# A gated outer-product recurrence and a token-channel mixer on one core: f loaded by token pairs, prefix sums from 64-row products, joint masks, scalings and exponentials

## The chip, the core and the metric

The kernel runs on 1 core of one Trainium2 chip. The metric is device time in microseconds (us) of one launch. Engines are named as in the profile: PE (TensorE matmuls), PEld (its weight loads), DVE (VectorE), ACT (ScalarE), POOL (GpSimd), SP (SyncE, which here only issues DMAs). PSUM has 8 banks of 512 float32 columns; the kernel hands them out by number.

## What is computed

For 4 batches of 768 tokens, 8 heads and 48 channels per head, a linear recurrence with a forget gate, and on its result a mixer over tokens and then over channels:

```python
f = 1.0 / (1.0 + np.exp(-f_logit))
for t in range(S):
    state = f[:, :, t, :, None] * state + np.einsum('bhd,bhe->bhde', k[:, :, t], v[:, :, t])
    y[:, :, t] = np.einsum('bhd,bhde->bhe', q[:, :, t], state)
x = y.transpose(0, 2, 1, 3).reshape(B, S, H * D)
h = np.maximum(x.transpose(0, 2, 1) @ w_tok1, 0.0) @ w_tok2
u = x + h.transpose(0, 2, 1)
out = u + np.maximum(u @ w_ch1, 0.0) @ w_ch2
```

## The kernel before

Each batch is cut into six chunks of 128 tokens. In a chunk, L = ln(1 + exp(-f_logit)) is made on ACT and split into a bfloat16 upper half (`Lhi`, a view) and a remainder (`Llo`, made by a subtraction on DVE or POOL). A product with a triangle of ones gives the prefix sums over the chunk's tokens in a PSUM bank. ACT turns the bank into the two gates G = exp(-sum) and Gi = exp(+sum); DVE scales q by G and k by Gi; PE transposes both; the copies out of PSUM are called *turned*. The score matmuls put a chunk's 8 heads into two banks, DVE multiplies them by the triangular mask, and two more products give y: *within* (masked scores by v) and *past* (q by the block-diagonal copy of the state, `state_bd`, which the helper `spread` makes). *parts* is k by v, the chunk's share of the next state. The result is copied out twice, as `x_bf` and `x_nat`. The mixer then runs *tok1* and *tok2* (over tokens), a transpose *ut*, and *ch1* and *ch2* (over channels), 288 matmuls of 128x384 per direction of the channel part over the whole kernel.

**Batch 0** goes by pairs of chunks (`pair(m)`, m = 0, 1, 2). Its loads put two consecutive tokens into each partition, so that partition t of column j holds token 2t + j of 256, and partitions 0 to 63 hold the first chunk of the pair, 64 to 127 the second. The masks for this layout are `pmask`. **Batches 1 to 3** go by `attention(b, (c, c + 1))` with one token per partition; there `sums_and_turns` makes the prefix sums by two matmuls of 128x384 per chunk (L461 with `Lhi`, L462 with `Llo`).

Nothing is scheduled at run time. The helper `add` records every operation with its engine, `ORDER` is a list of their numbers with an engine letter and the PSUM banks to use, and `plan.run` writes the instructions in that order. Each engine works through its own part of the list in order; semaphores between engines are put in when the program is built, from the tiles and the PSUM banks that two instructions share. So what matters around the change is the list and those waits. The DMAs of q, k, v, f of batch 1 and the weights are issued from POOL's part of the list (L266, L272), f of batch 0 and the stores from SP's.

Lines of before that the prediction uses: L392 and L388 make L of batch 0 and L371, L372 that of the others; L628 and L630 are G and Gi of batch 0; L637 scales q or k of batch 0, L490 both at once in the others; L644 transposes and L676 scores of batch 0; L706 is its mask; L665, L719 and L743 are parts, within and past of batch 0; L277 and L279 are copies on ACT and DVE; L413 and L500 are scores and transposes of the other batches; L757, L773, L826, L845 are tok1, tok2, ch1, ch2; L877 and L882 are idle matmuls at the start.

Of the kernel before, what the change touches and what calls it, by code (L numbers as in the profile page):

```python
# [28 lines left out]
HALVES = False  # L29
STATES = (DVE, POOL,)  # L30
# [6 lines left out]
w512 w512 w384 s19 32 20G 7G 33 8D 6G 10D 0D 34 11G 19D 1 5D 9G 2 24D 3A 27D 23A 18D 21G 22G 35 49 37 50 16G 51 36 52D  # L37
54 14D 13D 25D 12D 53G 26A 55 28 39 100:0 58 56D 105:1 40 57D 102 59 38 104 137:2 101 60D 142:3 42 108 107 61D 106 110
41 139 109 119:1:0 144 103 114:4 29D 143 62 111:5 125 138 115 112 116D 180:1 113A 130 146 126A 140 117:0:4 30A 127G
148:5 43 31A 149 141 175:2 181 147 121 145 150A 131G 118:3:6 120 44 151:0 176 123 156:5:4 182 17G 152 177 122 15G 153A  # L40
185 63 124:2:3 179 184 183 134 133A 178 189:6 64 132A 190 162 186:1 191A 187 4G 154:5:0 45 157 188A 163G 158 155:6:0 46
129A 169 193:1:5 164A 160 135A 47 128D 165A 192:4:6 159 339 65 336 197 161:2:0 337 170G 195 340 166 338G 198 342 194:5
173 172A 196 171G 358:1 343 341G 200 199:6:7 360 167D 359 201G 215:5 136D 204 361 216 203G 366:4 205D 202G 208:3 362
174A 217 68 363 209 206 367 210 168D 364:1 369 67 207D 211 218 345 212 365D 213 66 219 220 214A 374:2 221D 368 242 72
238 377 243 239 222:5 244D 234 241A 344G 235 226:1 240A 378 227 256:4 236A 230:3 70 254:6 257D 231 245A 228 252:2 394:4
255A 69 253D 223 346 248:7 232 290:6 249A 224 73 288:2 396 229 291A 284:7 233 347G 250:1 286:6 285A 251D 351 48 246:3
402:1 397 247D 300:7 225 76 352 289D 270:3 405 301D 264:5 74 272:2 406 237A 348 296:7 71 370 273D 268:0 349 398 271D 75
265A 292:2 269D 297A 276:3 371 287A 266:7 350D 403 258:6 353D 395 298:0 267A 81 277D 404 262:4 293A 372:3 439:2 373D
382:1 260:7 299D 79 375:5 261A 376:0 386 259A 78 304:7 263A 407 302:5 385 441 294:4 384A 379 280:6 295A 383D 381G 274:3
440 380G 387 278:4 399 431:0 281D 388G 282:2 432 275D 391:6 279A 469:1 283A 400:3 393D 433 408:4 392A 77 326:2 390A 409D  # L50
434 306:6 389G 303D 435 401D 327 305D 410:5 411:0 413 412:7 328 415 414 470 321:3 416D 436 417A 307 423 418G 82 437:5
424 419:0 329 462:7 83 422 322 421A 330 438A 420D 308 425G 427G 463 323 80 445:0 324 85 587 331:4 449 596 332 584 86 309
585 464 448 310 428:6 426G 590 311:0 87 429D 333 442 430A 84 586D 593 443:5 588 334 354 447:6 444D 602:3 454:4 605 450
471 451D 446:2 606 589D 594 316:6 604 457 312 452G 603 89 458 453A 610:5 591 607 472 465 88 611 459:2 595D 612 608:3
592D 455A 313 613 460D 466 615 473 597 474 456D 467 646:5 468A 598G 475D 317 647 314 609A 479:1 91 461D 482:7 488:0 480
649 476:2 483 616:4 481G 648 477 491:1 484G 599 638:7 489 95 478A 496:2 492 485:5 640 318 497D 617A 92 486 498:2 494:1
620:0 490G 499A 495D 618:5 319 600 90 619:1 622 493A 508:2 96 520:6 623 509A 630 518:5 639 601G 621 830 528:2 641 510:1
631 487G 521D 506:0 642 624G 821 629 625G 526:6 614 507A 94 519D 522:7 824 643 502:0 831 93 524:5 527D 529A 512:4 833
503D 97 635:2 818 513D 514:0 511A 98 819 504:4 516:6 505D 834 820D 644:1 356 517A 515D 500:4 525A 626:3 675:6 651 501A
554:5 678 637D 548:4 636D 679 677 652:0 632G 645D 628A 650 555 355 827 523D 676 653D 559:2 549A 627D 634A 546:6 656:4  # L60
547A 655:3 633G 659 825 654:7 822 836:6 657 556 823G 666 683:1 667 560 660G 685 832G 828 658 552:0 839 532:3 557 99
536:7 680 661A 684 713:5 662G 561 553A 686 838 542:1 537D 357 672:0 562 544:7 668 673D 663:2 545A 687:4 669D 543A 665D
843:7 837 538:1 674D 826G 846 533D 530:6 847 845 671G 714 534:3 531D 844 840 681:0 688D 539A 535A 706:7 707 664D 550:1
682D 540:2 551A 691:3 541A 689:6 694 690:1 670A 693 870:2 695G 574:3 692 873 697G 575 696G 702 874 829G 576 701 841 715
708 698:4 577 871 877:1 835D 709 703:3 848 569:0 699D 849 878 570 704D 872 700D 716 717 710 842 718 711 905:4 719D 712A
852:2 705A 732:5 558 855 879 735:7 320 880 856G 723:3 736 563 729:6 857A 726:1 733 881 737G 908 571 730 325 724 579:5
# [9 lines left out]
1006:0 983D 978:4 977D 996:1 1010:7 990:6 1011D 992:3 991D 968:7 997D 993A 1004:6 979D 1012:1 1005D 970:4 1015D 998:6  # L76
969D 986:5 973D 1002:7 999D 1000:2 971D 1003A 1008:6 1007D 987A 1046:7 1013D 1031:5 1001D 1036:1 1009D 1037 1041:6
1021:2 1047 1032 1048 1022 1038 1023 1039 1042 1049 1024 1050 1043 792 1026:2 1040 1016:7 1033 1017 1034 1027 1044 1035
1045 1028 1025 1018 1029 1030 1019 1020
"""  # L80


# [833 lines left out]
```

## Time and profile before

| | |
|---|---|
| median of 3 runs | 172.35 us (171.44 to 172.51) |
| the profiled execution | 172.62 us, its span 169.8 us |
| PE busy | 161.6 us of the span, 1757 matmuls |
| DVE, ACT, POOL busy | 130.1, 101.1, 86.7 us |
| mean granted TensorE clock | 0.976 |
| DMA | 89572 packets, 22.72 MB |

The span runs from the first to the last instruction; 2.8 us of the execution lie around it. The profile's page cuts the span into 40 slices of 4.2 us and gives the busy share of each engine in tenths. Three stretches can be told apart. In the first 25 us batch 0 is worked off by a chain over all engines, and PE has gaps. From there to 166 us PE is never idle: the mixer of one batch and the attention of the next are interleaved. The last 3.5 us are the last sum on DVE and the last stores.

### The profile page before, as it was taken

The numbers are of one execution on the slowest core, as the hardware profiler recorded it, in microseconds if no ns is written. First come the engines' busy times: TensorE is split into PE (matmuls) and PEld (weight loads), VectorE is DVE, ScalarE is ACT, GpSimd is POOL, SyncE is SP. The second block draws the span as 40 slices with busy tenths as digits, with TensorE's granted clock in tenths as the row PEclk, the third lists the DMA queues.
The fourth block names the chain that finished last, engine by engine and source line by source line (L and its number), as shares of the span: only waits on it lengthen the run. The fifth ranks groups of instructions, "written<-read, shape, count | busy, mean of one in ns | idle before, by whom it ended". The sixth has DMA issues, their size and how long they took to land.

```text
span 169.8 us, 4441 instructions
## 1 busy us (share of the span) xinstructions
PE 161.6 (95%) x1757; PEld 103.9 (61%) x1757; DVE 130.1 (77%) x282; ACT 101.1 (60%) x226; POOL 86.7 (51%) x125
## 2 busy tenths in 40 slices
PE   6799789999999999999999999999999999999991
PEld 2476556566676666666667665666657665666660
DVE  4389796998789799998989897999677426687222
ACT  3999997789671759999977737656541223112000
POOL 8899989899461997899989131110120010000000
PEclk9999956999999999999999999999999999999998
DMA  5999999999999999999999929995340033700044
GB/s 140 235 171 220 204 179 210 189 137 178 172 226 151 88 139 159 194 102 61 87 140 145 127 11 111 277 209 168 62 108 4 0 70 73 276 4 0 0 148 178
DMA packets 89572, 22.72 MB, mean 134 GB/s; under 512 B 82288, under 2 KB 88736, under 8 KB 89552
## 3 DMA queue, kind: packets, MB, share of 16 engines
q0 software_dynamic: 69600, 13.77, 95.6%
q1 hardware_dynamic: 19952, 8.69, 20.2%
q8 instruction: 13, 0.21, 0.5%
q14 instruction: 7, 0.06, 0.1%
HBM read 25.17 MB, written 4.72 MB: 176 GB/s over the span
## 4 chain that ended last, share of the span: by engine, by line
PE 88%; ACT 5%; DVE 2%; DMA 2%; issue 0%; DVEq 0%
PE ps L826 28%; PE ps L845 28%; PE ps L757 5%; PE ps L773 5%; PE ps L500 3%; PE ps L413 3%; PE ps L461 2%; PE ps L564 2%; DMA f_sb<-in_f_logit_dram 2%; PE ps L462 2%; PE ps L429 2%; PE ps L560 2%; DVE zT L706 1%; PE ps L644 1%; PE ps L719 1%; ACT f_sb L392 1%
## 5 line engine op out<-in xcount | busy, mean ns | idle before, releaser
L845 PE MATMUL ps<-w_ch,zT 128*128 128x384 bf16 (+2 forms) x300 | 52.1, 320 | 0.0
L826 PE MATMUL ps<-uT,w_ch 128*128 128x384 bf16 x288 | 52.0, 326 | 0.0
L845 PEld LDWEIGHTS <-zT 128*128 128x128 bf16 x300 | 28.0, 98 | 17.1
L826 PEld LDWEIGHTS <-w_ch 128*128 128x128 bf16 x288 | 27.2, 97 | 17.3
L357 ACT ACTIVATE zT<-ps 128x384 bf16<-128x384 f32 x48 | 22.3, 491 | 20.6 <-PE ps L826 16.8
L359 DVE TENSOR_SCALAR zT<-ps 128x384 bf16<-128x384 f32 x48 | 24.8, 550 | 2.8 <-PE ps L826 2.7
L541 DVE TENSOR_TENSOR AmT<-ps,tri_bf 128x512 bf16<-128x512 f32 x36 | 23.4, 683 | 0.9 <-PE ps L413 0.7
L851 DVE TENSOR_TENSOR x_nat<-x_nat,ps 128x384 f32<-128x384 f32 (+2 forms) x25 | 12.8, 533 | 11.4 <-PE ps L845 11.3
L281 POOL CAST state_bd<-state 48x192 bf16<-48x192 f32 x24 | 8.6, 357 | 23.9 <-DVE state L577 9.5
L266 POOL DMA_DIRECT2D qk_sb<-in_q_dram x16 | 15.6, 979 | 1.1 <-DMA w_ch<-in_moe_w_ch_dram 1.1
L266 POOL DMA_DIRECT2D v_sb<-in_v_dram x16 | 15.8, 990 | 0.5 <-DMA f_sb<-in_f_logit_dram 0.5
L266 POOL DMA_DIRECT2D qk_sb<-in_k_dram x16 | 16.0, 1000 | 0.1
L789 DVE TENSOR_TENSOR x_nat<-x_nat,ps 128x384 f32<-128x384 f32 x21 | 10.6, 548 | 4.9 <-PE ps L773 4.9
L757 PE MATMUL ps<-x_bf,w_tok 128*128 128x384 bf16 x48 | 13.0, 340 | 0.0
L279 DVE CAST x_bf<-ps 128x384 bf16<-128x384 f32 x18 | 9.9, 552 | 3.7 <-ACT x_nat L277 1.7
L281 POOL CAST u_bf<-x_nat 128x384 bf16<-128x384 f32 x8 | 4.3, 544 | 16.2 <-issue 11.4
L471 ACT ACTIVATE GG<-ps 128x384 bf16<-128x384 f32 x18 | 8.7, 489 | 5.2 <-DVE qk L490 3.6
L490 DVE TENSOR_TENSOR qk<-qk_sb,GG 128x768 bf16<-128x768 bf16 x18 | 10.0, 556 | 0.3 <-ACT GG L471 0.3
L773 PE MATMUL ps<-h1T,w_tok 128*128 128x384 bf16 x48 | 9.8, 326 | 0.0
L473 ACT ACTIVATE GG<-ps 128x384 bf16<-128x384 f32 x18 | 8.8, 491 | 1.6 <-PE ps L462 1.2
L379 POOL TENSOR_TENSOR Llo<-L 128x384 bf16<-128x384 f32 x10 | 8.3, 833 | 2.0 <-ACT L L372 2.0
L372 ACT ACTIVATE L<-f_sb 128x384 f32<-128x384 f32 x18 | 9.1, 523 | 0.2
(103 smaller groups left out, 262.0 us busy)
## 6 DMA issues: line engine op xcount, KB each, us to landing
out_dram<-x_nat SPq DMA_DIRECT2D x23, 192.0 KB, 2.2
f_sb<-in_f_logit_dram POOLq DMA_DIRECT2D x3, 1152.0 KB, 10.8
f_sb<-in_f_logit_dram SPq DMA_DIRECT2D x3, 384.0 KB, 4.2
qk_sb<-in_k_dram POOLq DMA_DIRECT2D x12, 96.0 KB, 7.4
qk_sb<-in_q_dram POOLq DMA_DIRECT2D x12, 96.0 KB, 6.2
w_ch<-in_moe_w_ch_dram POOLq DMA_DIRECT2D x2, 576.0 KB, 11.8
v_sb<-in_v_dram POOLq DMA_DIRECT2D x12, 96.0 KB, 5.1
w_ch<-in_moe_w_ch_dram POOLq DMA_DIRECT2D x1, 1152.0 KB, 9.5
```

The lines of the kernel that those rows point to most:

```text
L266: lambda eng=eng, into=into, of=of: eng.dma_start(out=into, in_=of),
L281: nc.gpsimd.tensor_copy(out_, in_)
L357: nc.scalar.activation(out_, in_, AF.Relu, bias=0.0, scale=1.0)
L359: nc.vector.tensor_scalar(out_, in_, 0.0, None, ALU.max)
L490: add(("gated", b, c, *names), DVE, lambda n=n: nc.vector.tensor_tensor(qk[it][:, n, :, 0:D], qk_sb[nb][:, n, :, c, :], GG[i][:, n], ALU.m ...
L541: add(("masked", b, c, p), DVE, lambda half=half, made=made: nc.vector.tensor_tensor(half, made(), tb4, ALU.mult), need=["tri_bf"], make=[ ...
L757: add(("tok1", b, rt, kt), PE, lambda rt=rt, kt=kt, pm=pm: nc.tensor.matmul(banks[pm.at][:, 0:DM], lhsT=w_tok1[:, kt, rt * 128:(rt + 1) * ...
L773: nc.tensor.matmul(banks[pm.at][:, 0:DM], lhsT=w_tok2[:, kt, tt * 128:(tt + 1) * 128], rhs=h1T[:, kt, :], start=(kt == 0 and not held), st ...
L789: nc.vector.tensor_tensor(to, un, banks[pm.at][:, 0:DM], ALU.add)
L826: nc.tensor.matmul(banks[pm.at][:, 0:384].rearrange("p (n t) -> p n t", t=128), lhsT=w[:, kt, c0:c0 + 128], rhs=uT[:, rows3, kt, :], start ...
L845: nc.tensor.matmul(banks[pm.at][:, 0:n1 - n0], lhsT=zT[:, kt, tt * 128:(tt + 1) * 128], rhs=w_ch2[:, kt, n0:n1], start=(kt == 0), stop=(kt ...
L851: add(("sum", b, tt, n0), DVE, lambda un=un, pm=pm, n=n1 - n0: nc.vector.tensor_tensor(un, un, banks[pm.at][:, 0:n], ALU.add), make=[("x_n ...
```

## The change

It has four parts and a new `ORDER`.

1. **f of batches 1 to 3** is loaded by token pairs like batch 0's (`FPAIR`): 384 contiguous bytes instead of 192, half as many descriptors.
2. **Their prefix sums** come from products of 64 rows. The upper 64 partitions of a column hold the first chunk of a pair, the lower 64 the second; the two triangles needed (`steps[:, 0]`, `steps[:, 1]`) are the masks that batch 0 already had. For two chunks there are 8 matmuls with 64 rows and 384 columns, alternately rows 0 to 63 into one bank and 64 to 127 into another, in place of 4 with 128 rows.
3. **In batch 0** the scaling of q and k of a chunk is one DVE instruction of 768 columns (`GATED2`), and the mask of a chunk one of 1024 columns over its two banks (`MASK2`).
4. **In pairs 1 and 2 of batch 0** G of both chunks is one ACT instruction over two banks, and Gi too (`EXP2`). For this `GG` is one tile, and all eight banks are one PSUM tile `ps`; two banks x < y are read as `psum[:, x:y + 1:y - x]`.

`HEADS`, `HALF0` and `COPIED` are off, so their branches make nothing.

```diff
+GATED2 = (0, 1, 2)
+MASK2 = (0, 1, 2)
+EXP2 = (1, 2)
+FPAIR = True
...
-w512 w512 w384 s19 32 20G 7G 33 8D 6G 10D 0D 34 11G 19D 1 5D 9G 2 24D 3A 27D 23A 18D 21G 22G 35 49 37 50 16G 51 36 52D
+w512 w512 w512 s7 32 18G 33 5D 20D 34 14D 7D 21D 0D 12D 1 6G 2 36 23D 3D 26D 24D 22G 27D 28 49 8D 13G 17D 35 29D 50 37
...
-    GG = [st([128, 2, H, D], BF16, f"GG{i}") for i in range(2)]
+    GG2 = st([128, 2, 2, H, D], BF16, "GG")
+    GG = [GG2[:, i] for i in range(2)]
...
-    banks = [ps.tile([128, 512], FP32, tag=f"ps{i}", name=f"ps_{i}") for i in range(NBANK)]
+    psum = ps.tile([128, NBANK, 512], FP32, tag="ps", name="ps")
+    banks = [psum[:, i] for i in range(NBANK)]
...
+            if b and n == "f" and FPAIR:
+                into = into.rearrange("t h (m j) d -> t h m (j d)", j=2)
+                of = src[b].rearrange("h (m t j) d -> t h m (j d)", t=C, j=2)
...
     def attention(b, cs):
         nb = b % NB
-        heads = [sums_and_turns(b, c) for c in cs]
+        p_s = [Bank(), Bank()]
+        if FPAIR:
+            c0 = cs[0]
+
+            def prefix():
+                for n, (t, j) in enumerate((t, j) for j in range(2) for t in (Lhi[b % 2][:, c0 + j], Llo[place(b, c0 + j)])):
+                    for k in range(2):
+                        rows = slice(64 * k, 64 * k + 64)
+                        nc.tensor.matmul(banks[p_s[k].at][:, 0:DM], lhsT=steps[rows, j, :], rhs=t[rows, :, 0:D],
+                                         start=(n == 0), stop=(n == 3))
...
+            def both(n, scale):
+                (x, y) = sorted(b.at for b in p_s)
+                of, for_ = psum[:, x:y + 1:y - x, 0:DM], GG2[:, :, n].rearrange("p j h d -> p j (h d)")
+                nc.scalar.activation(for_, of, AF.Exp, bias=0.0, scale=scale)
...
+            if m in GATED2:
+                add(("gated", 0, c), DVE, lambda j=j, c=c: nc.vector.tensor_tensor(
+                    qk[j][:, :, :, 0:D], qk_sb[0][:, :, :, c, :], GG[slot(j)], ALU.mult),
+                    need=[("q", 0, c), ("k", 0, c), ("G", j), ("Gi", j)], make=[("qh", j), ("kh", j)],
+                    kind=("el", 2 * DM, False, 2))
...
+            def masked(j=j):
+                x, y = p_a[j][0].at, p_a[j][1].at
+                nc.vector.tensor_tensor(
+                    ATp[i2][:, j].rearrange("p (r n) t -> p r n t", r=2),
+                    psum[:, x:y + 1:y - x].rearrange("s r (n t) -> s r n t", t=C),
+                    pmask[j].rearrange("s t j -> s (t j)").unsqueeze(1).unsqueeze(1).broadcast_to((128, 2, 4, C)), ALU.mult)
```

The new list gives these pairs of banks to the joint instructions of batch 0. Exponentials: 0 and 2 for pair 1, 0 and 6 for pair 2. Masks of chunks 1, 0, 3, 2, 4, 5, in their order on DVE: 4 and 5, 2 and 3, 1 and 6, 2 and 5, 1 and 4, 3 and 6.

What the list does to the order is shown at three places, each row with the semaphores that the instruction waits for; a semaphore is named after the engine that raises it (Activation is ACT). The first is ACT in before, at the exponentials of pair 2, which come in four instructions with the copies of pair 1 (`zT<-ps`) between and after them:

```order
L628 ACTIVATE GG_81<-ps_113 128x384 [waits DVE_49,PE_49]
L633 ACTIVATE gpair_121<-ps_115 128x8
L277 ACTIVATE zT<-ps_117 128x1024 [waits PE_49]
L628 ACTIVATE GG_80<-ps_114 128x384 [waits DVE_49,PE_49]
L630 ACTIVATE GG_81<-ps_113 128x384 [waits DVE_49]
L630 ACTIVATE GG_80<-ps_114 128x384
L277 ACTIVATE zT<-ps_112 128x1024 [waits DVE_49,PE_49]
```

The same place now, on ACT:

```order
L301 ACTIVATE zT<-ps 128x1024 [waits PE_49]
L301 ACTIVATE state_bd_96<-state 48x4x48 [waits DVE_49,Pool_49]
L301 ACTIVATE steps<-x_nat_100 64x64
L694 ACTIVATE GG<-ps 128x2x384 [waits DVE_49,PE_49]
L694 ACTIVATE GG<-ps 128x2x384 [waits PE_49,Activation_49]
L301 ACTIVATE zT<-ps 128x1024
L301 ACTIVATE zT<-ps 128x1024 [waits PE_49]
```

Two joint exponentials stand ahead of both copies of pair 1, and each has a wait for PE. Counted through the semaphores' raises in the compiled program, the first waits for the mask of chunk 1 on DVE (banks 4 and 5) and the scores of chunk 0 on PE (banks 3 and 2), the second for the transposes of k of chunks 2 and 3 on PE (bank 1); all these banks lie between 0 and 6.

The second place is DVE in before, from the third mask of pair 1 to the last of pair 2:

```order
L706 TENSOR_TENSOR zT<-ps_118,x_nat_101 128x512 [waits PE_49,Activation_49]
L279 CAST x_bf_102<-ps_114 128x384 [waits Activation_49]
L706 TENSOR_TENSOR zT<-ps_112,x_nat_101 128x512
L706 TENSOR_TENSOR zT<-ps_117,x_nat_101 128x512 [waits PE_49]
L706 TENSOR_TENSOR zT<-ps_118,x_nat_101 128x512 [waits PE_49]
L706 TENSOR_TENSOR zT<-ps_113,x_nat_101 128x512
L706 TENSOR_TENSOR zT<-ps_116,x_nat_101 128x512 [waits PE_49]
```

And DVE there now, from the mask of chunk 3 to that of chunk 5:

```order
L778 TENSOR_TENSOR zT<-ps,steps 128x1024 [waits PE_49,Activation_49]
L303 COPY zT<-ps 128x1024 [waits PE_49]
L778 TENSOR_TENSOR zT<-ps,steps 128x1024 [waits PE_49,Activation_49]
L778 TENSOR_TENSOR zT<-ps,steps 128x1024 [waits PE_49]
L846 TENSOR_TENSOR tsum<-state,ps 128x192 [waits PE_49,Pool_49]
L778 TENSOR_TENSOR zT<-ps,steps 128x1024 [waits PE_49]
```

Four joint masks stand where seven rows were; counted the same way, the first waits on ACT for the `x_nat` copy of chunk 0 (bank 2, between 1 and 6), the second for a turned copy of pair 2 (bank 4, between 2 and 5), the last on PE for *within* of chunks 2 and 3 (it writes banks 2 and 5; 5 lies between 3 and 6).

The third place is PE now, at the transposes of k of chunks 2 and 3, behind the scores of chunk 0:

```order
L760 MATMUL ps<-zT 64x128
L726 LDWEIGHTS qk_81 [waits DVE_49]
L726 MATMUL ps<-ident,qk_81 128x128 [waits Activation_49]
L726 LDWEIGHTS qk_81
L726 MATMUL ps<-ident,qk_81 128x128
```

In before the transposes of q of chunk 4 stood at the like place of the next pair, behind *past* of chunk 1:

```order
L743 LDWEIGHTS zT
L743 MATMUL ps_115<-state_bd_97,zT 128x96
L644 LDWEIGHTS qk_82 [waits DVE_49]
L644 MATMUL ps_118<-ident,qk_82 128x128
L644 LDWEIGHTS qk_82
```

The wait on ACT in the new rows is for the first joint exponential of pair 2 (banks 0 and 6), while the transposes write bank 1. On PE there also stand now: the transposes of k of chunks 4 and 5 (bank 3) with a wait for the mask of chunk 3 (banks 1 and 6); the scores of chunk 4 into bank 4 with a wait for the mask of chunk 2 (2 and 5); *within* of chunks 2 and 3, from bank 2 on, with one for the mask of chunk 4 (1 and 4); and *past* of chunk 3 (bank 5) with one for the mask of chunk 5 (3 and 6).

More of the change, by code (lines that the diff above doesn't have):

```diff
@@ L42 @@
[L42 to L46, printed above, removed]
@@ L204 @@
     tsum = st([128, HP, D], FP32, "tsum")
+    state_bf = [st([128, HP, D], BF16, f"state_bf{i}") for i in range(2)] if HEADS else None
     state_bd = [st([128, HP, 2 * D], BF16, f"state_bd{i}") for i in range(2)]
```

186 lines of the change are left out of this document (134 added, 52 removed).

## The prediction

> **What bounds the kernel now.** I read the page first, for the span and the slices.
>
> ```profile
> span 169.8 us, 4441 instructions
> PE   6799789999999999999999999999999999999991
> DVE  4389796998789799998989897999677426687222
> ACT  3999997789671759999977737656541223112000
> PEclk9999956999999999999999999999999999999998
> ```
>
> PE is full from the seventh slice to the last but one. So the end is set by when PE becomes full, by the work left for it then, and by its clock. Two digits of the clock, 5 and 6, stand in slices 6 and 7. The chain that ended last confirms it: from the first tok2 on it is PE alone, and it ends with one sum on DVE.
>
> ```profile
> 25.68 0.75 PE ps L719 x32
> 30.93 1.61 PE ps L773 x9
> 145.72 8.78 PE ps L826 x54
> 154.50 11.74 PE ps L845 x84
> 166.26 0.55 DVE x_nat L851
> ```
>
> Then the table by stretches, for the time ahead of that (columns: length, busy PE, PEld, DVE, ACT, POOL, clock).
>
> ```profile
> 10.00:15.00 5.00, 4.76 (x107) 3.57 (x104) 4.64 (x14) 4.88 (x15) 4.90 (x5) 1.00 2.01 173
> 15.00:20.00 5.00, 4.07 (x127) 3.08 (x125) 4.10 (x11) 4.96 (x10) 4.89 (x9) 1.00 1.13 239
> 20.00:25.00 5.00, 3.97 (x105) 3.02 (x105) 5.00 (x11) 4.67 (x12) 4.46 (x8) 0.66 1.84 176
> 30.00:35.00 5.00, 5.00 (x44) 2.88 (x43) 4.79 (x11) 4.11 (x11) 3.90 (x5) 1.00 1.90 175
> ...
> 19.50:20.00 0.50, 0.00 (x0) 0.00 (x0) 0.50 (x2) 0.50 (x2) 0.48 (x2) 1.00 0.90 183
> 21.50:22.00 0.50, 0.41 (x16) 0.40 (x15) 0.50 (x3) 0.42 (x2) 0.41 (x1) 0.61 1.57 187
> 28.00:28.50 0.50, 0.50 (x3) 0.25 (x2) 0.50 (x2) 0.32 (x1) 0.50 (x1) 0.56 1.12 210
> ```
>
> Batch 0 keeps ACT 98% busy (4.88 and 4.96 of 5) and then DVE 100%, while PE waits for them. They overlap well: that is what the order of before buys. The clock was at half from about 21.6 to 28.4 us, after a stretch in which PE stood still for half a microsecond and more, and it came back 5.8 us after PE had become steadily busy at 22.7.
>
> **The change, part by part.** I add up against the profiled execution, 172.62 us; the median is 0.27 less.
>
> *f by pairs* saves 9216 descriptors on POOL's queue. The load of batch 1 is used as it lands, and the wait for it was
>
> ```profile
> ACT f_sb L371 <- DMA f_sb<-in_f_logit_dram: 0.2, 1, 0.2
> f_sb<-in_f_logit_dram POOLq DMA_DIRECT2D x3, 1152.0 KB, 10.8
> ```
>
> 0.2 us. More is not to be had: bounds 0 and -0.2 us, and I take 0, because ACT reaches that place later now.
>
> *The prefix sums* cost PE 4 x 0.163 us for two chunks before (8.78 / 54 in the row of L826 above, products of the same 128x384). The price of 64-row products of 384 columns has no row. The nearest are the scores of batches 1 to 3, with 48 rows in the same alternation:
>
> ```profile
> 44.18 0.33 PE ps L413 x8
> 42.68 0.45 PE ps L500 x8
> 52.16 0.59 PE ps L413 x16
> 73.41 0.55 PE ps L413 x16
> ```
>
> Eight more take 0.22 to 0.26 us, 28 to 32 ns each, against 56 ns for full-height products of the same 128 columns (0.45 / 8). So two run side by side; a change of height costs the rest, 0.33 - 0.22 = 0.11 us. Eight in twos are 4 x 0.163 again. The order has 54 changes of height instead of 52: +0.2 us. If they ran one by one, nine pairs would cost 36 x 0.163 = 5.9 us more. I take 0.2.
>
> *The joint instructions.* Rows for the widths:
>
> ```profile
> L706 DVE TENSOR_TENSOR zT<-ps,x_nat 128x512 bf16<-128x512 f32 x12 | 7.6, 682 | 0.9 <-PE ps L676 0.9
> L789 DVE TENSOR_TENSOR x_nat<-x_nat,ps 128x384 f32<-128x384 f32 x21 | 10.6, 548 | 4.9 <-PE ps L773 4.9
> L628 ACT ACTIVATE GG<-ps 128x384 bf16<-128x384 f32 x6 | 2.9, 512 | 0.0
> L371 ACT ACTIVATE f_sb<-f_sb 128x384 f32<-128x384 f32 x18 | 8.9, 518 | 0.3 <-DMA f_sb<-in_f_logit_dram 0.2
> L392 ACT ACTIVATE f_sb<-f_sb 128x768 f32<-128x768 f32 x3 | 2.5, 833 | 1.8 <-DMA f_sb<-in_f_logit_dram 1.8
> L637 DVE TENSOR_TENSOR qk<-qk_sb,GG 128x384 bf16<-128x384 bf16 x12 | 3.7, 365 | 0.1
> L490 DVE TENSOR_TENSOR qk<-qk_sb,GG 128x768 bf16<-128x768 bf16 x18 | 10.0, 556 | 0.3 <-ACT GG L471 0.3
> 21.92 3.07 DVE L706 TENSOR_TENSOR zT<-ps,x_nat 128x512 bf16<-128x512 f32 x5
> ```
>
> A mask of 1024 columns: (682 - 548) / 128 = 1.05 ns a column, so 0.682 + 512 x 1.05 ns = 1.22 us; bounds 0.69 (one of 512) and 1.36 (two). A joint exponential: 0.512 + (833 - 518) ns = 0.83 us, bounds 0.51 and 1.02. Since five masks in a row took 3.07 us, 0.61 each, two cost 1.23: nothing is saved. Two scalings save 2 x 0.365 - 0.556 = 0.17, less the same overlap. The gain of all joint work is at most 0.5 us on each engine.
>
> *The waits.* Here lies the cost. A joint instruction on banks x and y is held in the compiled program as if it touched every bank between them, and what touches those banks later is held for it, read against read too. One bank shared by two readers is taken in turns already in before:
>
> ```profile
> DVE x_bf L279 <- ACT x_nat L277: 1.7, 1, 1.7
> ```
>
> I follow the new order with these rows beside those above:
>
> ```profile
> L277 ACT ACTIVATE zT<-ps 128x1024 bf16<-128x1024 bf16 x5 | 5.0, 1018 | 0.1
> L277 ACT ACTIVATE x_nat<-ps 128x384 f32<-128x384 f32 x13 | 6.4, 489 | 3.6 <-DVE x_bf L279 1.5 <-PE ps L564 1.3 <-PE ps L773 0.6
> L279 DVE COPY zT<-ps 128x1024 bf16<-128x1024 bf16 x1 | 0.7, 692 | 0.4 <-PE ps L644 0.4
> 12.00 0.55 ACT L628 ACTIVATE GG<-ps 128x384 bf16<-128x384 f32 x1
> 17.05 0.67 PE L719 MATMUL ps<-v_sb,zT 64*128 64x48 bf16 x32 [0.20 <-ACT GG L630]
> 22.66 0.97 PE L719 MATMUL ps<-v_sb,zT 64*128 64x48 bf16 x31 [0.27 <-DVE zT L706]
> 20.13 0.42 PE L676 MATMUL ps<-zT 48*64 48x128 bf16 x16 [0.86 <-DVE zT L706]
> 21.59 0.64 PE L676 MATMUL ps<-zT 48*64 48x128 bf16 x16 [0.44 <-DVE zT L706]
> ```
>
> Handing over costs about 0.06 us between ACT and DVE, and 0.23 after a PE group. Pair 1's exponentials ended at 12.55; now I put them at 13.0. DVE must then do the turned copy of k (0.69, held back until the joint exponential on banks 0 and 2 is done, since it reads bank 1), state, tsum and two joint scalings, 2.45 with its bubbles, and the mask of chunk 1: 13.0 + 2.45 + 1.22 = 16.7. From there each step waits for the one ahead:
>
> first exponential of pair 2, 0.9: 17.6; transposes of k, 0.68: 18.3; second exponential, 0.83: 19.1; mask of chunk 0, 1.28: 20.4; within and past, 0.84 + 0.23: 21.5; on ACT x_nat, spread, x_bf, x_nat, 1.7: 23.2; mask of chunk 3, 1.28: 24.5; transposes and turned copy of k of pair 2 on PE and DVE, 1.45 (ACT's copy of q, 1.03, lies beside it): 26.0; mask of chunk 2, 1.22: 27.2; scores of chunks 4 and 5, 0.84 + 0.3: 28.3; mask of chunk 4, 1.22: 29.5; within, 0.9: 30.4; mask of chunk 5, 1.28: 31.7; past of chunk 3, two tok1 and the pair's sums, which stand ahead of it on PE, 1.2: 32.9.
>
> There within of the last pair starts, which in before ended its wait at 25.6 (the row of L719 x32 above). Until tok2 PE then has 3.5 us of work (within 0.7, past 0.3, ten tok1 1.6, transposes 0.45, scores 0.3): 36.4 against 30.93, a loss of 5.5 us. Behind the waiting PE group stand all of the mixer's matmuls, and behind POOL's spread of chunk 3 the loads of w_ch1's second half and of v; PE's list after tok2 is as long as before (the same 672 products of 384 columns in the mixer).
>
> *The clock.* In this stretch PE works some 6 of 16 us, less than between 20 and 25 us in before, so I expect half speed from about 20 us. By the two pairs of rows (0.42 to 0.64, 0.67 to 0.97) small groups then take 1.5 times as long, wide ones twice: on the chain within and past +0.4, transposes +0.45, scores +0.4, within and past +0.4, tok1 and sums +1.0, together 2.7 us. PE is steadily busy from about 33.3; if the clock returns 5.8 us later, as before, 3.4 us after the late within run at half, 1.7 us lost. Sum: 172.62 + 5.5 + 2.7 + 1.7 = 182.5, and 0.27 less for the median: **182.2 us**.
>
> **Rivals.**
>
> *The clock stays up.* Then 172.35 + 5.5 = 177.9 us. For it: no single PE gap of my chain is much over 2.5 us. Against it: the clock fell in before with less idling. The Trainium skill, "TensorE: Matmul & The Clock Gate", section "Why this matters for your kernels", says that the clock drops where PE idles for more than about 3 us between bursts; by that rule it would stay up here and the time be 177.9. The trace differs: no gap ahead of 21.6 us was longer than 0.9.
>
> *The holds cost nothing* (the faster side): each waited-for instruction is done by the time its waiter is reached, so only true data sets the chain. Then masks and exponentials overlap as in before: DVE's masks end at about 24.8 instead of 25.0, and PE has by then done 0.65 us more for the mixer and half a microsecond less idling, 172.35 - 1.3 = 171.0 us. It decides if the exponential of pair 2 starts before the mask of chunk 1 has ended. Against it stands the order of DVE, where that mask comes after both scalings that wait for the same exponentials. The skill's "Advanced Engine Details and Errata", section "Bank Collisions", lets ACT and DVE read PSUM at once where their banks differ; by it the holds for banks between are not needed by the chip, and without them the time would be this rival's. The compiled program has them all the same.
>
> *The prefix products run one by one*: 182.2 + 5.9 = 188 us. The L413 rows speak against it.
>
> *The loads come too late*: w_ch1's second half and v of batch 1 are issued behind the late spread; I find 1 to 4 us of slack, and put a miss at 2 us, 184.
>
> **Chances.** Forecast 0.58; clock up 0.2; loads late 0.07; one by one 0.06; holds free 0.09. The range takes in the first three with the bounds of the mask (six on the chain, -3.2 or +0.8 us) as far as they are likely: from 176.5 (clock up, masks a little cheaper) to 186.0 (loads late, half speed from 17 us, masks dearer). That leaves out 0.15. A measurement tells 1% (1.7 us) from no change. Holds free at 171.0 is 0.8% below, so it gives 0.05 to the same and 0.04 to faster; all else, 0.91, is slower.
>
> **What would show it.** Right: idle ACT of about 2 us ahead of the first joint exponential of pair 2, ended by a mask; DVE gaps ahead of the masks, ended by ACT; within of the last pair at 33 to 37 us; the first tok2 near 40; half clock from 20 to 39 us; from tok2 to the end as long as before; a pair's sums in 0.65 to 0.8 us. Wrong: the last mask before 27 us, or a stall of PE after 45 us.

## The result, and the profile after

The changed kernel takes 182.02 us (median of 4 runs, 181.15 to 183.04) against 172.43 us of the kernel before beside it (171.44 to 173.38). The ratio is 1.056, with a 95% interval of 1.047 to 1.065: slower, by 9.6 us. Here and below a ratio and its interval compare fast runs alone, while a median takes in every run, so the two can differ by some tenths of a per cent. The profiled execution took 181.41 us, its span 179.6 us.

The page of the changed kernel, the rows that answer to those shown of before:

```profile
span 179.6 us, 4464 instructions
PE   6994766899999999999999999899999999999992
DVE  7856665499688578799899986897573573271232
ACT  3994776477848789899999807749677021532200
PEclk9999655599999999999999999999999999999999
```

PE becomes full two slices later than before, and between slices 4 and 8 no engine is full: DVE stands at 4 to 6 where it had 6 to 9. Four digits of the clock instead of two are at or near half. So the time was lost by engines that wait for each other. DVE's own list shows for whom. These are the masks and what stands ahead of the first (columns: start, length, engine, line, operation, count, and in brackets the idle time ahead and what ended it):

```profile
14.30 1.02 DVE L714 TENSOR_TENSOR qk<-qk_sb,GG 128x768 bf16<-128x768 bf16 x2
15.24 1.22 DVE L778 TENSOR_TENSOR zT<-ps,steps 128x1024 bf16<-128x1024 f32 x1
18.96 1.23 DVE L778 TENSOR_TENSOR zT<-ps,steps 128x1024 bf16<-128x1024 f32 x1 [2.50 <-ACT GG L694]
23.60 1.22 DVE L778 TENSOR_TENSOR zT<-ps,steps 128x1024 bf16<-128x1024 f32 x1 [0.46 <-PE ps L726]
26.58 1.23 DVE L778 TENSOR_TENSOR zT<-ps,steps 128x1024 bf16<-128x1024 f32 x1
28.96 1.23 DVE L778 TENSOR_TENSOR zT<-ps,steps 128x1024 bf16<-128x1024 f32 x1 [1.15 <-PE ps L760]
31.10 1.23 DVE L778 TENSOR_TENSOR zT<-ps,steps 128x1024 bf16<-128x1024 f32 x1 [0.65 <-PE ps L829]
```

The mask of chunk 0 starts 2.5 us after that of chunk 1 has ended, although its scores (PE, 14.44 to 15.08) were long done: ACT's two joint exponentials and a group of transposes have slipped between them. In before the last six masks, of 512 columns each, stood one behind the other with one copy between, until 24.99; now the last one ends at 32.33. The lists of ACT and of PE have the other members of the ring:

```profile
16.55 0.81 ACT L694 ACTIVATE GG<-ps 128x768 bf16<-128x768 f32 x1 [1.87 <-DVE zT L778]
18.11 0.81 ACT L694 ACTIVATE GG<-ps 128x768 bf16<-128x768 f32 x1 [0.75 <-PE ps L726]
```

```profile
17.41 0.61 PE L726 MATMUL ps<-ident,qk 128*128 128x128 bf16 x8 [2.33 <-ACT GG L694]
18.98 1.01 PE L726 MATMUL ps<-ident,qk 128*128 128x128 bf16 x8 [0.96 <-ACT GG L694]
...
34.68 0.85 PE L829 MATMUL ps<-v_sb,zT 64*128 64x48 bf16 x32
...
38.14 1.50 PE L888 MATMUL ps<-h1T,w_tok 128*128 128x384 bf16 x8
```

ACT's first exponential starts when the mask of chunk 1 ends, PE's transposes when that exponential ends, ACT's second when the transposes end. *Within* of the last pair (L829) and the first tok2 (L888) follow at 34.7 and 38.1 us, where before had them at 25.6 and 30.9. In the table by stretches (length, PE, PEld, DVE, ACT, POOL, clock), the clock falls just ahead of 19 us and is back at 36:

```profile
18.50:19.00 0.50, 0.03 (x1) 0.02 (x1) 0.04 (x1) 0.50 (x2) 0.50 (x1) 0.96 1.76 190
25.00:30.00 5.00, 3.24 (x72) 2.59 (x71) 2.93 (x3) 4.82 (x10) 2.01 (x3) 0.50 1.38 164
36.00:36.50 0.50, 0.50 (x7) 0.37 (x6) 0.50 (x1) 0.48 (x2) 0.50 (x2) 0.97 2.35 120
```

From the start of the first tok2 to the last sum, before and after (one row of each kernel's table):

```profile
30.93:166.26 135.33, 135.30 (x1288) 86.42 (x1288) 106.92 (x222) 74.93 (x171) 57.93 (x77) 1.00 1.12 119
```

```profile
38.14:176.10 137.96, 137.30 (x1331) 86.31 (x1328) 97.62 (x202) 87.53 (x200) 52.48 (x69) 1.00 1.02 117
```

So some 7.2 us were lost ahead of tok2 and 2.6 us behind it, together the 9.8 us between the spans of the two profiled executions (169.8 and 179.6 us). A part of the second is one stall of PE, behind a store and a small load on SP's queue:

```profile
113.98 0.81 PE L960 MATMUL ps<-w_ch,zT 128*128 128x384 bf16 x4 [0.50 <-DVE x_nat L904]
```

```profile
109.57 0.42 SPq L970
110.10 2.89 DMA glast<-grow
113.11 0.36 DVE state L603
113.47 0.47 DVE x_nat L904
```

### The profile page after: what moved, and what is told of

Read it like the earlier page. It is cut to its first block, busy times and chain, and to the rows that moved or that the text cites. A ratio compares the mean times of both kernels' runs of the same rounds, so it can differ in the third digit from the quotient of the medians.

```text
span 179.6 us, 4464 instructions
## 1 busy us (share of the span) xinstructions
PE 165.5 (92%) x1781; PEld 105.0 (58%) x1781; DVE 123.0 (68%) x255; ACT 112.3 (63%) x247; POOL 79.7 (44%) x115
## 3 DMA queue, kind: packets, MB, share of 16 engines
q0 software_dynamic: 69600, 13.77, 85.9%
## 4 chain that ended last, share of the span: by engine, by line
PE 79%; DVE 11%; ACT 4%; issue 2%; DMA 2%; SPq 0%; POOL 0%; DVEq 0%; ACTq 0%
PE ps L941 25%; PE ps L960 24%; PE ps L453 4%; PE ps L872 4%; PE ps L888 4%; DVE zT L778 3%; PE ps L554 3%; PE ps L468 3%; PE ps L726 2%; ACT GG L694 2%; PE ps L618 2%; DMA glast<-grow 2%; PE ps L484 1%; PE ps L614 1%; PE ps L678 1%
## 5 line engine op out<-in xcount | busy, mean ns | idle before, releaser
L381 ACT ACTIVATE zT<-ps 128x384 bf16<-128x384 f32 x64 | 28.5, 491 | 19.7 <-PE ps L941 18.0
L383 DVE TENSOR_SCALAR zT<-ps 128x384 bf16<-128x384 f32 x32 | 17.2, 553 | 10.3 <-PE ps L941 10.2
L305 POOL CAST state_bd<-state 48x192 bf16<-48x192 f32 x20 | 7.0, 348 | 19.5 <-DVE state L631 8.4
L301 ACT ACTIVATE x_nat<-ps 128x384 f32<-128x384 f32 x16 | 7.8, 494 | 9.0 <-DVE x_bf L303 6.6
L301 ACT ACTIVATE state_bd<-state 48x192 bf16<-48x192 f32 x20 | 7.2, 360 | 8.9 <-DVE state L631 8.2
L872 PE MATMUL ps<-x_bf,w_tok 128*128 128x384 bf16 x48 | 12.4, 337 | 0.0
L631 POOL TENSOR_TENSOR state<-tsum,glast 128x192 f32<-128x192 f32 x5 | 2.5, 502 | 21.2 <-ACT zT L381 17.8
L303 DVE CAST x_bf<-ps 128x384 bf16<-128x384 f32 x16 | 8.8, 553 | 4.4 <-PE ps L857 2.4
L778 DVE TENSOR_TENSOR zT<-ps,steps 128x1024 bf16<-128x1024 f32 x6 | 7.3, 1224 | 4.8 <-ACT GG L694 2.5
L527 ACT ACTIVATE GG<-ps 128x384 bf16<-128x384 f32 x18 | 8.8, 494 | 1.7 <-PE ps L453 1.5
```

The costliest lines, as they stand in the source:

```text
L301: nc.scalar.activation(out_, in_, AF.Copy, bias=0.0, scale=1.0)
L305: nc.gpsimd.tensor_copy(out_, in_)
L381: nc.scalar.activation(out_, in_, AF.Relu, bias=0.0, scale=1.0)
L383: nc.vector.tensor_scalar(out_, in_, 0.0, None, ALU.max)
L778: nc.vector.tensor_tensor(ATp[i2][:, j].rearrange("p (r n) t -> p r n t", r=2), psum[:, x:y + 1:y - x].rearrange("s r (n t) -> s r n t", t=C),
L872: add(("tok1", b, rt, kt), PE, lambda rt=rt, kt=kt, pm=pm: nc.tensor.matmul(banks[pm.at][:, 0:DM], lhsT=w_tok1[:, kt, rt * 128:(rt + 1) * ...
```

## Experiments

The theory: an instruction that reads two banks x and y is held as if it touched the banks between, and these false waits put batch 0 into a row. The main rival: the new order itself, or the wide instructions, are at fault. Each kernel is the changed one but for the edit shown, except where it is said to be the one before; the median of before measured beside it is given with each time, and line numbers shift by one or two with an edit.

### One bank at a time: all, masks alone, exponentials alone

```diff
-                nc.scalar.activation(for_, of, AF.Exp, bias=0.0, scale=scale)
+                for i, bank in enumerate((x, y)):
+                    nc.scalar.activation(GG2[:, i, n].rearrange("p h d -> p (h d)"), psum[:, bank, 0:DM],
+                                         AF.Exp, bias=0.0, scale=scale)
...
-                    psum[:, x:y + 1:y - x].rearrange("s r (n t) -> s r n t", t=C),
+                for p, bank in enumerate((x, y)):
+                    nc.vector.tensor_tensor(
+                        ATp[i2][:, j, 4 * p:4 * p + 4, :], psum[:, bank].rearrange("s (n t) -> s n t", t=C),
```

Both edits:

> Each joint exponential and each joint mask of batch 0 is issued as two instructions of one bank, at the same place of the same list, with the same banks. Theory (holds through the banks between): the false waits are gone, the two instructions cost 0.15 to 0.2 us more than the joint one, 10 times; within of the last pair starts at 26 to 28 us instead of 34.7, the clock is at half for 10 us at most, and the time is 174.5 us (173 to 176.5); it stays above 172.4 because 2.6 us of the loss lie behind the first tok2. Rival (the new order itself is the loss, whatever the width of the instructions): above 180 us, within of the last pair still behind 33 us.

Only the second:

> Only the masks are issued as two instructions of one bank; the exponentials of pairs 1 and 2 stay joint. Theory: the holds behind 18.9 us go, those of the exponentials on banks 0 and 6 stay, so the mask of chunk 0 still starts near 19 us and the rest of the chain runs without waits; 177 us (175 to 179). Rival (the order is the loss): above 180 us.

Only the first:

> Only the exponentials are issued as two instructions of one bank; the masks stay joint. Theory: the mask of chunk 0 follows that of chunk 1 at once, near 16.6 instead of 19.0 us, and the later chain stays, so 2.5 us are won and a part of the half clock: 179 us (177 to 180.5). Rival (the order is the loss): above 180.5 us, mask of chunk 0 still near 19 us.

Measured, with before at 171.87 us: 173.9 us for both (ratio 1.007, interval 1.002 to 1.011), 176.36 for the masks alone (1.024, 1.018 to 1.029), 178.03 for the exponentials alone (1.034, 1.029 to 1.039). The list of operations and the banks are those of the changed kernel, and there are more instructions, not fewer; yet of the 9.6 us over before only 1.2 are left by the ratio (2.0 by the medians). Each part alone removes its own waits and leaves the other's. With the exponentials single, the first two masks follow at once, two in one row:

```profile
14.45 2.36 DVE L779 TENSOR_TENSOR zT<-ps,steps 128x1024 bf16<-128x1024 f32 x2 [0.28 <-PE ps L761]
```

With the masks single and the exponentials joint, the wait for ACT ahead of the mask of chunk 0 is there as in the changed kernel:

```profile
19.46 1.29 DVE L779 TENSOR_TENSOR zT<-ps,steps 128x512 bf16<-128x512 f32 x2 [2.92 <-ACT GG L694]
```

### The same joint instructions on neighbouring banks

Nothing but bank numbers in the list is changed, for the operations of batch 0 and the first ones behind it; the exponentials of pair 1 get 6 and 7, those of pair 2 0 and 1, the masks 6 and 7, 2 and 3, 3 and 4, 0 and 1, 3 and 4, 6 and 7. One of the six rows of the list that change:

```diff
-115:3:2 127G 119 168 143:1 144 129G 167 128G 44 118 140:4 145A 141 148:6:5 63 152 142A 120:2:3 153D 64 130 171 132A
+115:3:2 127G 119 168 143:4 144 129G 167 128G 44 118 140:5 145A 141 148:6:1 63 152 142A 120:2:7 153D 64 130 171 132A
```

> The changed kernel, with all joint instructions and the same order; only the banks of batch 0 are given out anew, so that the two banks of every joint exponential and mask are neighbours and no bank lies between. Theory (holds through the banks between): as with single instructions, 173 us (172 to 175), the mask of chunk 0 behind that of chunk 1 without a gap, within of the last pair at 24 to 28 us. Rival (a joint access is slow or late by itself, wherever its banks are): 178 us or more.

173.77 us, with before at 172.03 (1.007, 1.003 to 1.011): the wide instructions are as good as single ones when no bank lies between. This, with the three kernels above, shows the cause of the greater part: of the 9.6 us some 8.4 go with the distance of the two banks, and neither the order nor the width needs them. The 1.2 us that stay (ratio 1.007, with neighbouring banks as with single instructions) have other causes, taken up below.

```profile
14.45 2.36 DVE L778 TENSOR_TENSOR zT<-ps,steps 128x1024 bf16<-128x1024 f32 x2 [0.28 <-PE ps L760]
19.12 1.22 DVE L778 TENSOR_TENSOR zT<-ps,steps 128x1024 bf16<-128x1024 f32 x1
20.85 2.35 DVE L778 TENSOR_TENSOR zT<-ps,steps 128x1024 bf16<-128x1024 f32 x2
23.37 1.22 DVE L778 TENSOR_TENSOR zT<-ps,steps 128x1024 bf16<-128x1024 f32 x1
```

The last mask ends at 24.59, where before had 24.99. ACT's joint exponentials of pair 2 now run beside the first two masks:

```profile
14.29 1.51 ACT L694 ACTIVATE GG<-ps 128x768 bf16<-128x768 f32 x2 [0.36 <-DVE qk L714]
```

### The clock's share

Idle matmuls, whose results nobody reads, fill PE's gaps in batch 0: z8 stands for eight of 512 columns, s8 for eight of 64. One of the three rows of the list that change:

```diff
-115:3:2 127G 119 168 143:1 144 129G 167 128G 44 118 140:4 145A 141 148:6:5 63 152 142A 120:2:3 153D 64 130 171 132A
+115:3:2 127G 119 168 z8 143:1 144 129G 167 128G 44 118 z3 140:4 145A 141 148:6:5 63 152 142A s8 120:2:3 153D 64 130 171 132A
```

> The changed kernel, with idle matmuls of 512 columns (8, 3, 2, 4, 4, 3, 3 of them, and 8 short ones) put into PE's gaps between 15 and 32 us; they write bank 7, which is free until within of the last pair. They are shorter than the gaps. This measures the clock's share of the loss. Theory: the clock stays full through the chain, the holds stay, first tok2 at 35 to 36.5 us instead of 38.1, time 179.2 us (177.9 to 180.5). Rival (the half clock costs nothing, since the holds set the chain): 181.5 to 182.5 us; the sum of the prediction (4.4 us for the clock) would give 177.6.

177.91 us, with before at 172.03 (1.035, 1.030 to 1.039). The clock stayed full in the profiled execution, the false waits stayed (the mask of chunk 0 still waits 2.50 us for ACT), and the first tok2 moved from 38.14 to 35.33:

```profile
PEclk9999999999999999999999999999999999999999
```

```profile
19.12 1.23 DVE L778 TENSOR_TENSOR zT<-ps,steps 128x1024 bf16<-128x1024 f32 x1 [2.50 <-ACT GG L694]
```

```profile
35.33 1.46 PE L888 MATMUL ps<-h1T,w_tok 128*128 128x384 bf16 x8
```

So the half clock cost 2.8 us ahead of tok2. Behind it the stalls of PE did not occur in this execution, which is 0.6 us more (137.3 us from there to the last sum, 172.66 - 35.33, against 137.96). Together that is the 3.4 us between the two spans (179.6 and 176.2); the medians differ by 4.1 us, and what makes the rest isn't known.

### The prefix sums

The products get full height again, but over the columns as they lie, so the sums they make are not those of one chunk; only the time is of use.

```diff
-                    for k in range(2):
-                        rows = slice(64 * k, 64 * k + 64)
-                        nc.tensor.matmul(banks[p_s[k].at][:, 0:DM], lhsT=steps[rows, j, :], rhs=t[rows, :, 0:D],
-                                         start=(n == 0), stop=(n == 3))
+                    for k in ((n // 2,)):
+                        nc.tensor.matmul(banks[p_s[k].at][:, 0:DM], lhsT=steps[:, j, :], rhs=t[:, :, 0:D],
+                                         start=(n % 2 == 0), stop=(n % 2 == 1))
```

> The prefix sums of batches 1 to 3 are made by 4 matmuls with 128 rows in place of 8 with 64 (each chunk's from one column of both halves, so that the values are no prefix sums of a chunk). f keeps its layout. If the 64-row products cost what the chain shows in the full stretch (0.76 us for two chunks against 0.65), 8 or 9 pairs save 0.9 to 1.2 us: 181.0 us. By the sum of the prediction (+0.2 us in all) 181.8 us. If f's layout or the prefix were a main part of the loss, it would fall by several us.

180.93 us, with before at 171.87 (1.051, 1.047 to 1.056). The number is the expected one, the reason isn't. In the trace, from the start of the first of these products to the start of what follows, 8 pairs behind tok2 take 6.0 us with full height and 5.8 with 64 rows (5.5 in before): no gain. What is missing is the stall behind SP, because the same small load was issued in 0.48 us instead of 1.27, landed 1.9 us after its issue instead of 2.9, and so came in time:

```profile
110.03 0.48 SPq L534 DMA_DIRECT2D glast<-grow x1
```

The interval overlaps with that of the changed kernel (1.047 to 1.065), so the 1.1 us between the medians are not a finding. The 64-row products are not dear: a pair takes some 0.72 us in the full stretch.

### f as before the change

On the kernel with neighbouring banks:

```diff
-FPAIR = True
+FPAIR = False
```

The list is the same but for its numbers, which shift since a pair's sums are two operations again.

> The kernel with neighbouring banks, in which f of batches 1 to 3 is loaded as before the change (one token per partition) and the prefix sums are made by 4 full-height matmuls again; the list is the same. This undoes the first two parts of the change. By the prediction (prefix +0.2 us, the load worth nothing): 173.6 us, between 172.9 and 174.2. If the shorter load of f were worth more, it is slower, 174.5 us or above; if the 64-row products were dear, 172.5 us.

174.47 us, with before at 172.28 (1.014, 1.010 to 1.018); the kernel with neighbouring banks had 1.007 (1.003 to 1.011). It is slower, not faster, though the two intervals still touch. The load of f stands ahead of the last v on POOL's queue. By rows of one token POOL issues it in 2.29 us instead of 1.49, it lands after 11.6 us instead of 9.7, and that v after 9.9 instead of 8.1, so *parts* of the last pair waits for v:

```profile
23.34 0.62 PE L747 MATMUL ps<-v_sb,qk 64*64 64x48 bf16 x16 [1.16 <-DMA v_sb<-in_v_dram]
```

ACT waits for f itself too, off the chain that ended last:

```profile
22.38 0.94 ACT L395 ACTIVATE f_sb<-f_sb 128x384 f32<-128x384 f32 x2 [1.31 <-DMA f_sb<-in_f_logit_dram]
```

So f by pairs, with its prefix sums, was worth some 1.2 us in this list by the ratios, where I had allowed 0.2 for f. The halved descriptors don't show in the count of packets, which is 69600 on POOL's queue in both; they show in the issue and the landing.

### Why the neighbours are still not faster: a stop at a fixed matmul

With neighbouring banks the first tok2 starts at 30.16 us, already ahead of before's 30.86. What keeps the kernel behind lies after it: 137.8 us from there to the last sum (167.95 - 30.16) against 135.4. But ahead of tok2, too, time is left. With all holds gone, PE stands still in the middle of *within* of pair 1, for nothing that the profile names ("issue"). The first row is the kernel with single instructions, the second that with neighbouring banks:

```profile
23.40 0.62 PE L830 MATMUL ps<-v_sb,zT 64*128 64x48 bf16 x26 [0.80 <-issue]
```

```profile
23.67 0.50 PE L829 MATMUL ps<-v_sb,zT 64*128 64x48 bf16 x26 [1.30 <-issue]
```

Both stop behind the 351st matmul of the program. Two kernels put more idle matmuls at the start, so that this count falls elsewhere. The first is the kernel with neighbouring banks:

```diff
-w512 w512 w512 s7 32 18G 33 5D 20D 34 14D 7D 21D 0D 12D 1 6G 2 36 23D 3D 26D 24D 22G 27D 28 49 8D 13G 17D 35 29D 50 37
+w512 s28 s28 s7 32 18G 33 5D 20D 34 14D 7D 21D 0D 12D 1 6G 2 36 23D 3D 26D 24D 22G 27D 28 49 8D 13G 17D 35 29D 50 37
```

> The kernel with neighbouring banks, in which two of the three wide idle matmuls at the start (0.85 us each) become 28 short ones each (0.8 us), 54 matmuls more, with no other change. In the kernel with neighbouring banks PE stands still for 1.3 us in the middle of within of pair 1, behind its 351st matmul, without any wait that the profile shows, and a 16 KB instruction load lands about then; the kernel with single instructions stops at the same matmul. Theory (PE has run out of loaded instructions at a fixed number of matmuls): the stop moves to 54 matmuls earlier in the program, beside PE's wait for the mask of chunk 3, and is hidden there; within of the last pair starts about 1 us earlier, 172.7 us (172 to 173.5). Rival (it is a wait on data that the profile doesn't name): the stop stays at the same matmul of within, 173.8 us.

171.46 us (171.05 to 171.74), with before at 172.28: ratio 0.995, interval 0.993 to 0.998. That is below the range I had expected; it beats both kernels, if by little. The stop in *within* is gone, the clock is full throughout in the profiled execution, and *within* of the last pair starts at 24.97 (26.05 with neighbouring banks alone). What is left of it is hidden, if anywhere, behind the 349th matmul, where PE waits for a copy on ACT, not for a mask as I had written.

```profile
21.22 0.64 PE L760 MATMUL ps<-zT 48*64 48x128 bf16 x32 [1.07 <-ACT zT L301]
22.33 0.57 PE L829 MATMUL ps<-v_sb,zT 64*128 64x48 bf16 x32 [0.22 <-DVE zT L778]
24.97 0.58 PE L829 MATMUL ps<-v_sb,zT 64*128 64x48 bf16 x32
```

The control gives before the same treatment:

```diff
-w512 w512 w384 s19 32 20G 7G 33 8D 6G 10D 0D 34 11G 19D 1 5D 9G 2 24D 3A 27D 23A 18D 21G 22G 35 49 37 50 16G 51 36 52D
+w512 s28 s21 s19 32 20G 7G 33 8D 6G 10D 0D 34 11G 19D 1 5D 9G 2 24D 3A 27D 23A 18D 21G 22G 35 49 37 50 16G 51 36 52D
```

> The control to the kernel with neighbouring banks and 54 more idle matmuls, which is 0.8 us below before: the kernel before, in which the second and third wide idle matmul of the start become 28 and 21 short ones, 47 matmuls more. In before, too, PE has a gap at its 350th matmul (22.2 to 22.7 us), of which 0.27 us is a wait for a mask. If moving the stop is all that made the other kernel faster, before gains as much: 171.2 us or less. If the joint instructions with neighbouring banks carry it, before gains at most the part of the gap that is no wait, 0.2 us: 172.1 us (171.7 to 172.6).

171.65 us, with before at 172.3 (0.998, 0.995 to 1.001): not told apart from before, and its interval overlaps with that of the other; the time lies between what the two theories gave. So the gain of 0.8 us is real for the whole kernel, but how much of it the joint instructions carry stays open. A part comes with the clock. Over all experiments about half of the runs of before have a mean granted clock of 0.99 (171.8 us on average) and half of 0.98 (172.5 us), while the kernel with neighbouring banks and 54 more matmuls has 0.99 in six of twelve (171.6 us) and 1.00 in five (171.1 us). At 0.99, before with 47 more matmuls takes 171.5 us (seven runs), as little as the other. The gap at that place in before's list is still there, and it is a wait for a mask:

```profile
22.74 0.56 PE L719 MATMUL ps<-v_sb,zT 64*128 64x48 bf16 x31 [0.42 <-DVE zT L706]
```

### Three attempts on the kernel before

Joint scalings alone, for chunks 1 to 5, at the place of the earlier one of q and k:

```diff
+                    qk[j][:, :, :, 0:D], qk_sb[0][:, :, :, c, :], GG[j], ALU.mult) if first else nc.vector.tensor_tensor(
```

> The kernel before, where only the scalings of q and k of chunks 1 to 5 of batch 0 become one instruction, at the place of the earlier one. DVE saves 5 times 0.17 us ahead of its masks. If DVE bounds the end of batch 0: 171.5 us, 0.4 less than before; if the waits on ACT for the second gate take it back, as before.

172.36 us, with before at 172.03 (1.004, 1.001 to 1.007): no gain. The gaps on DVE moved: the third pair of masks waits 1.3 us for its scores instead of 0.9, and starts at 20.97 instead of 19.39. The first row is before:

```profile
19.39 1.29 DVE L706 TENSOR_TENSOR zT<-ps,x_nat 128x512 bf16<-128x512 f32 x2 [0.87 <-PE ps L676]
```

```profile
20.97 1.29 DVE L708 TENSOR_TENSOR zT<-ps,x_nat 128x512 bf16<-128x512 f32 x2 [1.32 <-PE ps L678]
```

Of this delay the joint scalings, which wait for both gates, are at most a part. In the profiled execution a small copy on DVE took 1.88 us where before had 0.19, and ended when POOL's issue of the load of f ended (11.46 to 13.73 us); what held it was not tested.

```profile
11.87 1.88 DVE L279 COPY x_nat<-x_nat 128x128 bf16<-128x128 bf16 x1
```

Idle matmuls in the gaps of before (the first of two rows of the list that change):

```diff
-185 63 124:2:3 179 184 183 134 133A 178 189:6 64 132A 190 162 186:1 191A 187 4G 154:5:0 45 157 188A 163G 158 155:6:0 46
+185 63 124:2:3 179 184 183 134 133A 178 189:6 64 132A 190 162 186:1 191A 187 4G 154:5:0 45 157 188A 163G 158 z3 s4 155:6:0 46
```

> The kernel before, with 4 idle matmuls of 512 columns and 18 of 64 in PE's gaps between 19.3 and 22.7 us, to bank 7. If PE's idling there is what halves the clock from 21.6 to 28.4 us, one or both of the two windows go and the time falls by 1 to 2 us, to 170.2 us. If the clock follows something else, as before (171.9).

172.94 us, with before at 172.03 (1.007, 1.003 to 1.011): a miss. The clock stayed full in the profiled execution, as intended, but the fillers brought PE's 350th matmul into a run without waits, and it stopped there:

```profile
23.24 0.35 PE L676 MATMUL ps<-zT 48*64 48x128 bf16 x10 [1.13 <-issue]
```

The first tok2 came only 0.2 us earlier (30.67), and 1.4 us were lost behind it (167.48 - 30.67 = 136.8 against 135.4), half of them in a wait for a DMA far from batch 0:

```profile
146.77 3.42 PE L826 MATMUL ps<-uT,w_ch 128*128 128x384 bf16 x20 [0.75 <-DMA uT<-u_bf]
```

And the same with 31 idle matmuls for one wide one at the start:

```diff
-w512 w512 w384 s19 32 20G 7G 33 8D 6G 10D 0D 34 11G 19D 1 5D 9G 2 24D 3A 27D 23A 18D 21G 22G 35 49 37 50 16G 51 36 52D
+w512 s31 w384 s19 32 20G 7G 33 8D 6G 10D 0D 34 11G 19D 1 5D 9G 2 24D 3A 27D 23A 18D 21G 22G 35 49 37 50 16G 51 36 52D
```

> The kernel before with idle matmuls in PE's gaps, in which one of the wide idle matmuls at the start becomes 31 short ones. With the gaps filled, the clock was full throughout, but PE stood still for 1.1 us behind its 350th matmul, and the time was 0.9 us above before. If that stop is the instruction load, it moves to 30 matmuls earlier in the program, where the waits on the masks hide a part of it: 171.9 us (171 to 172.5). If it is a wait on data: 172.9 us, stop at the same instruction.

174.26 us, with before at 172.28 (1.006, 1.002 to 1.011): a miss in time. In the profiled execution the work of batch 0 came late as a whole, behind a wait of DVE for k (0.78 us at 14.71), and ran in part at half clock (24.9 to 31.7 us). But the stop moved as a count would have it. It isn't at its old instruction; PE's gap at the 350th matmul is now a wait for a copy, and a new stop stands 128 matmuls later, within the last pair:

```profile
28.35 0.27 PE L719 MATMUL ps<-v_sb,zT 64*128 64x48 bf16 x4 [0.93 <-issue]
```

## Why the prediction was right

The time, 182.02 against 182.2 us, is closer than the reasoning deserves: two terms were off by nearly the same amount, in opposite directions, and that is luck. I had 9.9 us ahead of tok2 (5.5 for the chain, 4.4 for the clock) and nothing behind it; measured were some 7.2 and 2.6.

- **The waits: right, place by place.** The chain by hand had the mask of chunk 1 end at 16.7 (measured 16.46), the first exponential of pair 2 at 17.6 (17.36), the transposes at 18.3 (18.02), the second exponential at 19.1 (18.92), the mask of chunk 0 at 20.4 (20.19), that of chunk 3 at 24.5 (24.82), of chunk 2 at 27.2 (27.81), of chunk 4 at 29.5 (30.19), of chunk 5 at 31.7 (32.33). The last four hold a part of the half clock that I had summed apart, so they agree better than they should: with the clock kept full these four masks end at 24.25, 26.77, 28.72 and 30.62, and my steps were too long by up to 1.1 us. The experiments with single instructions and with neighbouring banks show the cause.
- **The durations: right.** A mask of 1024 columns took 1.22 us (1.22 put down), a joint exponential 0.81 (0.83), two scalings 0.51 each (0.56).
- **The chain and the clock: too dear.** At full clock I had *within* of the last pair at 32.9 and tok2 at 36.4; the kernel with filled gaps has them at 31.93 and 35.33. So 1.0 of the 1.1 us lies ahead of *within*, and the stretch from there to tok2 was right (3.5 and 3.4 us). For the half clock I took 4.4 us; it cost 2.8 ahead of tok2, with the start and the end of the half speed (20 us and later than 36) put a little late: it fell at 18.97 and was back at 36.03. I had let it run on for 5.8 us after PE became steadily busy; it was back 3.7 us after that (32.3 to 36.0). The first tok2 was forecast near 40 and came at 38.14.
- **"From tok2 to the end as long as before": wrong, by 2.6 us.** 0.5 to 0.65 of it is the stall behind SP's queue, which I had ruled out ("a stall of PE after 45 us" stood among the signs against me). Without a stall the new list takes 137.3 us there (171.46-us kernel: 165.76 - 28.45; kernel with filled gaps: 137.3) against 135.3, some 2.0 us; before with shifted matmuls has 135.9. I had taken the list behind tok2 to be as long as before and given the products of the mixer as the reason. Eight more scores behind tok2 are 0.28 us of it (0.55 us for 16) and the prefix sums 0.3 (5.8 - 5.5). The other 1.4 us are spread over small steps of the new order; what makes them was not settled.
- **The prefix sums: right in size** (+0.2 put down, +0.3 by the trace), and the rival that they run one by one is out.
- **f by pairs, put at 0: too low in this list.** Undone, together with the prefix sums, it costs some 1.2 us, and on the chain that ended last by the wait for v, not by that for f.
- **The sums.** The 0.2 us taken for the prefix sums never entered the total; with them it is 182.4. The work until tok2 adds up to 3.35, not 3.5, and 0.3 of it are scores that the new list has behind tok2. The gain of the rival without holds adds up to 1.15, not 1.3.

Of the rivals, "the clock stays up" was put at 177.9 us, and the kernel in which it was made to stay up takes 177.91. "The holds cost nothing" was put at 171.0; the kernel without holds and without the stop takes 171.46. Both are near partly by luck, since neither had the 2.0 us behind tok2. The loads of the fourth rival came in time: no wait of PE behind 28 us is for a DMA.

The rule on the clock from the Trainium skill, "TensorE: Matmul & The Clock Gate", section "Why this matters for your kernels", a drop where PE idles for more than about 3 us between bursts, is not borne out as a limit here: the longest gap ahead of the drop at 18.97 was 2.33 us. The Trainium skill, "Advanced Engine Details and Errata", section "Bank Collisions", has ACT and DVE read PSUM at once where their banks differ, and the kernel with neighbouring banks agrees: two masks take 2.36 us there while ACT's two exponentials run beside them, against 1.23 us for one mask alone.

## What to carry to other kernels

When one instruction is to read two PSUM banks, ask what the program's own dependence tracking will take it to touch, and give it neighbouring banks; count the semaphore waits in the compiled order before and after, since a wait that no data needs looks like any other. Where a chain over several engines falls apart, first write it down from the waits and the durations of before; that gave each mask here within 0.7 us, or within 1.1 at equal clock. And when a kernel is freed of its waits, look for the next thing that PE runs into: it may be in no part of the change.

## What was not expected of the hardware

- **A stop of PE at a fixed count of matmuls.** In four kernels PE stood still for 0.8 to 1.3 us behind its 350th or 351st matmul, or in one its 478th, wherever the program had them, if it came there through a run of small matmuls without waits. The profile names no wait. 128 matmuls with their weight loads are 256 instructions; the profile's instruction queue moves 16 KB a time (14 packets, 0.23 MB), which are 64 bytes for each of 256, and such a load starts 2.2 to 2.7 us ahead of the end of each stop (in the kernel with neighbouring banks the load starts at 21.17, PE stops at 22.4 and goes on at 23.67). That PE ran out of loaded instructions fits all of it, and moving the count moved the stop; it was not shown by itself.

```profile
q8 instruction: 14, 0.23, 0.5%
```

- **The half clock comes in pieces.** Until PE's work ended, its stretches were 3.4, 6.8, 10.2, 13.7 and 17.1 us long in the profiled executions, one to five times 3.41 us, and filling gaps of at most 2.3 us was enough to avoid it.
- **64-row products run two at a time.** Of each two, one on the upper and one on the lower rows, the second starts about 5 ns behind the first, and the pair takes 0.18 us, one of full height 0.17.
